# Context matmuls of a sliding-block attention kernel: streaming 194 columns instead of 193

## Chip, cores and metric

One core of one Trainium2 chip runs the whole program. The metric is the device time of one execution in microseconds; the kernel before takes 921.08 us (median of three runs, 920.9 to 921.36).

## The reference

A layer norm feeds two branches, attention against a cache (32 heads of 192, the last 512 cached positions) and a gated feed-forward block; their product is added to the input.

```python
W = min(4096, max(256, Sk // 4))                      # 512
q = (x @ wq).reshape(B, Sq, 32, 192).transpose(0, 2, 1, 3)
k, v = k_cache[:, :, Sk - W:, :], v_cache[:, :, Sk - W:, :]
scores = einsum("bhqd,bhkd->bhqk", q, k) * 192 ** -0.5
p = softmax(scores)
o = einsum("bhqk,bhkd->bhqd", p, v)                    # the context product
s = o.transpose(0, 2, 1, 3).reshape(B, Sq, 32 * 192) @ wo
...
return x + s * silu(((silu(xn @ w_gate)) * (xn @ w_up)) @ w_down)
```

## The kernel before

Heads are worked in 16 pairs. The softmax is not normalised until after the context product. The V tile has a column of ones behind the 192 columns of each head, so that the same matmul that forms the context also forms the sum of the row; the context is then divided by it. The tile has two columns of ones (194 columns per head), but only the first is streamed: 193 columns.

```python
V_p = consts.tile([P, KC, 2, Dh + 2], bf, name="V_p")      # KC = 4 chunks of 128 rows, 2 heads
...
nc.gpsimd.memset(V_p[:, :, :, Dh : Dh + 2], 1.0)           # once; the loads fill 0:Dh
...
def part(p):                                               # pairs 0 to 13: two 64-row halves at a time
    ...
    for kc in range(KC):
        for n, r in enumerate((lo, hi)):                   # rows 0-63 and 64-127 of the array
            k = n ^ turn
            qt = 2 * q2 + k
            m = nc.tensor.matmul(                          # L487
                acc[:, k, h * 256 : h * 256 + Dh + 1],
                Ps[i][kc][r, h, qt * P : (qt + 1) * P], V_p[r, kc, h, 0 : Dh + 1],
                start=(p == 0 and kc == 0), stop=(turn == 1 and kc == KC - 1),
                skip_group_check=True,
            )
...
def divide(i, q2, acc, by_dve):
    a_v = acc[:, :, :].rearrange("p k (h c) -> p k h c", h=2)
    nc.vector.reciprocal(r[:], a_v[:, :, :, Dh : Dh + 1])  # column 192
    ...                                                    # columns 0 to 191, scaled by r
...
def pv_full(i, q2):                                        # pairs 14 and 15: the full array
    ...
    nc.tensor.matmul(                                      # L539
        acc[:, k, h * 256 : h * 256 + Dh + 1],
        Ps[i][kc][:, h, qt * P : (qt + 1) * P], V_p[:, kc, h, 0 : Dh + 1],
        start=(kc == 0), stop=(kc == KC - 1),
    )
```

The softmax here doesn't subtract the row's maximum and nothing guards it: scores larger than these inputs give would overflow.

## Time and profile before

| | before |
|---|---|
| time | 921.08 us |
| matmul engine busy | 914.2 us, 99% of the span |
| context matmuls | 3584 of 64 rows (1792 side-by-side pairs) and 256 of 128 rows: 2048 slots |
| one slot, start to start | 83.5 ns |
| their share of the chain | 16% and 2% |

The prediction below shows the lines. A "slot" is the word used throughout for the time that one full matmul, or one pair of 64-row matmuls, holds the array. It is read from start times: from the start of a stretch of context matmuls to the start of whatever the engine does next, divided by the slots in between. Single start times stand in the trace to 1 ns; the timeline view rounds them to 10 ns. Unless said otherwise, a slot below is the median over all stretches of a kind. The tables of slots and gaps are worked out from these single start times; no view of the profile prints them, and differences under 1 ns do not show in the timeline lines of a short stretch.

### The profile page before, as it was taken

What the parts mean: (1) busy time and instruction counts of PE and PEld (TensorE: products, weight loads), DVE (VectorE), ACT (ScalarE), POOL (GpSimd) and SP (SyncE); (2) the same over time, 40 slices, a digit from 0 to 9 for tenths busy, and PEclk for the clock granted to TensorE, in tenths of its full rate; (3) what the DMA queues carried; (4) which work ended last, traced back from release to release, by engine and by line L of the source; (5) the groups of instructions that cost most, each with busy time, mean ns of one, the idle gap of its engine ahead of it and who ended that gap; (6) DMA issues with size and microseconds to landing.
All of it is one profiled execution on the core that took longest, in us unless ns stands there. A gap on an engine that the chain in (4) does not pass through costs nothing.

```text
span 919.1 us, 23174 instructions
## 1 busy us (share of the span) xinstructions
PE 914.2 (99%) x9920; PEld 548.9 (60%) x9920; DVE 601.8 (65%) x844; ACT 473.9 (52%) x840; POOL 85.2 (9%) x269
## 2 busy tenths in 40 slices
PE   9999999999999999999999999999999999999998
PEld 6444444465757575656565656566666666665665
DVE  6443321467677777777777777676867777777657
ACT  4222222557464646565656565655555555556471
POOL 0000000000000000000000000000000000001976
PEclk9999999999999999999999999999999999999999
DMA  9412430045352534253534343435243444443525
GB/s 299 79 35 64 92 82 0 1 75 112 54 113 50 111 51 108 54 108 54 108 58 109 57 108 52 110 53 108 56 87 73 90 77 75 91 71 102 120 59 166
DMA packets 248167, 77.53 MB, mean 84 GB/s; under 512 B 228993, under 2 KB 248065, under 8 KB 248065
## 3 DMA queue, kind: packets, MB, share of 16 engines
q1 hardware_dynamic: 245696, 73.39, 38.9%
q10 hardware_dynamic: 2368, 2.67, 0.9%
q8 instruction: 77, 1.26, 0.6%
q14 instruction: 26, 0.20, 0.1%
HBM read 38.93 MB, written 2.62 MB: 45 GB/s over the span
## 4 chain that ended last, share of the span: by engine, by line
PE 99%; DMA 1%; DVE 0%; ACTq 0%; issue 0%
PE mm L448 22%; PE sc L462 18%; PE mm L487 16%; PE sc L602 15%; PE sc L282 11%; PE mm L312 6%; PE sc L572 4%; PE sc L564 2%; PE mm L539 2%; PE mm L564 1%; DMA x_t<-in_A_x_dram 1%; PE gu L282 0%; PE mm L321 0%; PE sc L487 0%; PE sc L539 0%; PE mm L462 0%
## 5 line engine op out<-in xcount | busy, mean ns | idle before, releaser
L466 ACT ACTIVATE p_t<-sc 128x1024 bf16<-128x1024 f32 x254 | 252.9, 1022 | 120.5 <-PE sc L462 120.5
L453 DVE TENSOR_REDUCE qT<-mm 128x512 bf16<-128x1024 f32 x189 | 231.1, 1223 | 99.0 <-PE mm L448 96.5
L517 ACT ACTIVATE O_b<-mm,r 128x192 bf16<-128x192 f32 x486 | 164.6, 421 | 183.7 <-issue 136.9
L448 PE MATMUL mm<-xnT,wq_p 64*128 64x512 bf16 x1890 | 237.5, 376 | 0.0
L462 PE MATMUL sc<-qT,khat 64*128 64x512 bf16 x1524 | 198.0, 376 | 0.0
L487 PEld LDWEIGHTS <-p_t 64*128 64x128 bf16 x3584 | 159.3, 93 | 33.8
L487 PE MATMUL mm<-V_p,p_t 64*128 64x193 bf16 x3520 | 176.7, 242 | 0.0
L615 DVE TENSOR_TENSOR s_m<-s_m,sc 128x1024 f32<-128x1024 f32 x108 | 131.9, 1221 | 60.7 <-PE sc L602 52.3
L602 PE MATMUL sc<-wo_p,OT_b 64*128 64x512 bf16 x1296 | 168.8, 376 | 0.0
L448 PEld LDWEIGHTS <-wq_p 64*128 64x128 bf16 x1890 | 105.0, 94 | 98.9 <-issue 0.8
L462 PEld LDWEIGHTS <-khat 64*128 64x128 bf16 x1536 | 85.3, 94 | 80.4 <-DVE s_t L615 0.3
L602 PEld LDWEIGHTS <-OT_b 64*128 64x128 bf16 x1296 | 70.1, 94 | 44.1 <-issue 0.3
L615 DVE TENSOR_TENSOR s_t<-s_t,sc 128x512 f32<-128x512 f32 x108 | 74.2, 687 | 28.4 <-PE sc L572 26.6
L589 POOL MEMSET turn_t<- 128x1 f32 x220 | 21.6, 98 | 700.2 <-PE mm L487 506.2
L290 DVE TENSOR_TENSOR hT<-sc,sg 128x512 bf16<-128x512 f32 x46 | 31.7, 692 | 81.5 <-ACT sg L289 81.5
L289 ACT ACTIVATE sg<-sc 128x512 bf16<-128x512 f32 x46 | 27.3, 596 | 69.8 <-PE sc L282 69.8
L282 PE MATMUL sc<-xnT,wu_sb 128*128 128x512 bf16 (+1 forms) x260 | 60.5, 355 | 0.0
L282 PE MATMUL sc<-xnT,wg_sb 128*128 128x512 bf16 (+1 forms) x260 | 60.3, 355 | 0.1
L572 PE MATMUL sc<-OT_b,wo_p 64*128 64x512 bf16 (+1 forms) x345 | 50.3, 376 | 0.0
L312 PE MATMUL mm<-wd_sb,hT 128*128 128x512 bf16 x192 | 43.9, 379 | 0.0
L282 PEld LDWEIGHTS <-wu_sb 128*128 128x128 bf16 x285 | 27.2, 98 | 26.8 <-issue 0.2
L282 PEld LDWEIGHTS <-wg_sb 128*128 128x128 bf16 x285 | 27.2, 98 | 26.3
(83 smaller groups left out, 418.8 us busy)
## 6 DMA issues: line engine op xcount, KB each, us to landing
wo_p<-in_A_wo_dram SPq DMA_DIRECT2D x16, 480.0 KB, 4.8
K_p<-in_A_k_cache_dram SPq DMA_DIRECT2D x32, 192.0 KB, 4.6
V_p<-in_A_v_cache_dram SPq DMA_DIRECT2D x32, 192.0 KB, 3.6
wq_p<-in_A_wq_dram SPq DMA_DIRECT2D x64, 80.0 KB, 2.9
wq_p<-in_A_wq_dram SPq DMA_DIRECT2D x16, 160.0 KB, 3.2
x_t<-in_A_x_dram SPq DMA_DIRECT2D x13, 160.0 KB, 3.2
x_b<-in_A_x_dram SPq DMA_DIRECT2D x4, 512.0 KB, 6.4
OT_b<-O_b SPq DMA_TRANSPOSE x124, 2.8
```

Source lines behind the costliest of these rows:

```text
L282: nc.tensor.matmul(out, w_sb[:, c, f * P : (f + 1) * P], xnT[:, c, qc], start=(c == 0), stop=(c == NC - 1),)
L290: nc.vector.tensor_tensor(hTs[b][:, f, :], u, sg[:], ALU.mult)
L312: nc.tensor.matmul(dn, at, by, start=(f == 0), stop=(f == NF - 1))
L448: nc.tensor.matmul(q_ps[:, h, :], pairs[pr]["wq"][r, c, j * P : (j + 1) * P], xnT[r, c, b * 512 : (b + 1) * 512], start=(c == 0), stop=(c ...
L453: nc.vector.reduce_sum(qTs[i][:, j, :], q_ps[:, :, :].rearrange("p h n -> p n h"), axis=AX.X)
L462: nc.tensor.matmul(sc[:, h, :], khat[r, j, ks], qT[r, j, :], start=(j == 0), stop=(j == 2))
L466: nc.scalar.activation(p_t[:, :, :], sc[:, :, :], ACT.Exp, scale=scale)
L487: m = nc.tensor.matmul(acc[:, k, h * 256 : h * 256 + Dh + 1], Ps[i][kc][r, h, qt * P : (qt + 1) * P], V_p[r, kc, h, 0 : Dh + 1], start=(p ...
L517: nc.scalar.activation(O_b[:, qt, h, :], a_k[:, h, 0:Dh], ACT.Copy, scale=r[:, k, h, :])
L572: nc.tensor.matmul(ps.rearrange("p (t q) -> p t q", q=P), pairs[i // NB]["wo"][r, j, MC:D], OTs[i][:, :, :].rearrange("p (t j) q -> p j t ...
L602: m = nc.tensor.matmul(ps[:, k, :], OTs[i][r, 3 * (2 * half + k) + j, :], pairs[i // NB]["wo"][r, j, MAIN], start=(turn == 0 and j == 0), ...
L615: nc.vector.tensor_tensor(to, to, ps, ALU.add)
```

## The change

The intent is to stream both columns of ones, so that the width is even. The second one is computed and never read.

```diff
-                        acc[:, k, h * 256 : h * 256 + Dh + 1],
-                        Ps[i][kc][r, h, qt * P : (qt + 1) * P], V_p[r, kc, h, 0 : Dh + 1],
+                        acc[:, k, h * 256 : h * 256 + Dh + 2],
+                        Ps[i][kc][r, h, qt * P : (qt + 1) * P], V_p[r, kc, h, 0 : Dh + 2],
...   (the same two lines in pv_full)
```

More of the change, by code (lines that the diff above doesn't have):

```diff
@@ L539, in pv_full @@
                     nc.tensor.matmul(
-                        acc[:, k, h * 256 : h * 256 + Dh + 1],
-                        Ps[i][kc][:, h, qt * P : (qt + 1) * P], V_p[:, kc, h, 0 : Dh + 1],
+                        acc[:, k, h * 256 : h * 256 + Dh + 2],
+                        Ps[i][kc][:, h, qt * P : (qt + 1) * P], V_p[:, kc, h, 0 : Dh + 2],
                         start=(kc == 0), stop=(kc == KC - 1),
```

## The prediction

> **What bounds the kernel now.** I read the page first: the busy shares, the clock row, and the chain of work that ended last.
>
> ```profile
> PE 914.2 (99%) x9920; PEld 548.9 (60%) x9920; DVE 601.8 (65%) x844; ACT 473.9 (52%) x840; POOL 85.2 (9%) x269
> ...
> PEclk9999999999999999999999999999999999999999
> ...
> PE 99%; DMA 1%; DVE 0%; ACTq 0%; issue 0%
> PE mm L448 22%; PE sc L462 18%; PE mm L487 16%; PE sc L602 15%; PE sc L282 11%; PE mm L312 6%; PE sc L572 4%; PE sc L564 2%; PE mm L539 2%; PE mm L564 1%; DMA x_t<-in_A_x_dram 1%; PE gu L282 0%; PE mm L321 0%; PE sc L487 0%; PE sc L539 0%; PE mm L462 0%
> ```
>
> The reader is to see three things. The matmul engine is busy 99% of the span at full granted clock, so its cycles are the time. The chain says the same independently of busy time: 99% of the end-to-end path is matmul followed by matmul. And the two lines that the change edits, L487 (row-tiled context product) and L539 (full-array context product of the last two head pairs), are 16% and 2% of that path. There is nothing to hide a longer matmul behind, and nothing that would swallow a shorter one. So the question is only how long one of these matmuls holds the array at 193 columns and at 194.
>
> Next the groups of instructions with shapes kept apart, for counts.
>
> ```profile
> L487 PE MATMUL mm<-V_p,p_t 64*128 64x193 bf16 x3520 | 176.7, 242 | 0.0
> L539 PE MATMUL mm<-V_p,p_t 128*128 128x193 bf16 x224 | 20.8, 246 | 0.0
> L487 PE MATMUL sc<-V_p,p_t 64*128 64x193 bf16 x64 | 3.3, 242 | 0.0
> L539 PE MATMUL sc<-V_p,p_t 128*128 128x193 bf16 x32 | 2.8, 246 | 0.0
> L487 PEld LDWEIGHTS <-p_t 64*128 64x128 bf16 x3584 | 159.3, 93 | 33.8
> ```
>
> L487 runs 3520 + 64 = 3584 times, always as two 64-row halves side by side, that is 1792 pairs; L539 runs 224 + 32 = 256 times. That makes 1792 + 256 = 2048 slots of the array. The 242 and 246 ns are one instruction's time from start to its modelled end and overlap with the next, so they are not the price of a slot. The price is start to start, which I take from the timeline of the matmul engine (first column start, second length, both in us).
>
> ```profile
> 885.23 2.84 PE L539 MATMUL mm<-V_p,p_t 128*128 128x193 bf16 x32
> 887.91 2.83 PE L539 MATMUL sc<-V_p,p_t 128*128 128x193 bf16 x32
> 890.58 1.50 PE L539 MATMUL mm<-V_p,p_t 128*128 128x193 bf16 x16
> 891.92 1.46 PE L564 MATMUL sc<-wo_p,OT_b 128*128 128x512 bf16 x6
> ```
>
> ```profile
> 282.52 0.85 PE L487 MATMUL mm<-V_p,p_t 64*128 64x193 bf16 x16
> 283.19 1.47 PE L602 MATMUL sc<-wo_p,OT_b 64*128 64x512 bf16 x12
> ...
> 285.79 1.51 PE L487 MATMUL mm<-V_p,p_t 64*128 64x193 bf16 x32
> 287.13 0.83 PE L572 MATMUL sc<-OT_b,wo_p 64*128 64x512 bf16 x6
> ```
>
> Full array: 891.92 - 885.23 = 6.69 us for 80 matmuls, 83.6 ns each. Row pairs: 287.13 - 285.79 = 1.34 us for 16 pairs, about 83.75 ns each at this rounding. Single start times in the trace are finer: nearly every stretch of 16 full matmuls or 16 pairs takes 1336 ns and every stretch of 8 pairs 668 or 669 ns, so a slot is 83.5 ns, the same in both forms.
>
> For comparison the timeline gives other widths on the full array.
>
> ```profile
> 150.75 5.34 PE L312 MATMUL mm<-wd_sb,hT 128*128 128x512 bf16 x24
> 155.93 1.24 PE L321 MATMUL mm<-xnT,wq_p 128*128 128x512 bf16 x5
> ...
> 910.16 0.49 PE L564 MATMUL mm<-wo_p,OT_l 128*128 128x256 bf16 x3
> ...
> 915.08 0.49 PE L564 MATMUL sc<-wo_p,OT_b 128*128 128x256 bf16 x3
> ```
>
> 512 columns: 5.18 us / 24 = 215.8 ns. 256 columns: 4.92 us over fifteen groups of three, 109.3 ns (the finer starts mostly read 109). The slope is (215.8 - 109.3) / 256 = 0.416 ns a column, with about 2.5 ns per matmul on top (215.8 - 512 x 0.4167 = 2.5).
>
> **What the Trainium skill says.** "TensorE: Matmul & The Clock Gate", section "Wait — 56ns, not 53.3ns?", gives start to start of back-to-back matmuls at full clock as N / 2.4 GHz plus about 2.5 ns. The trace agrees at 512 (215.8 against 215.8) and 256 (109.2 expected, 109.3 read). At 193 it does not quite: 80.4 + 2.5 = 82.9 ns expected, 83.5 measured. The section "Back-to-back issue gap" of the same page offers about 131 ns per matmul as a sustained rate at N = 512; no full-array matmul here does that, so I don't use it.
> "PSUM — Partial Sum Buffer", section "Specifications (TRN2)", lists cachelines of 8 bytes, which is two fp32 output columns. No run here shows that yet, but it would make 193 columns, 772 bytes, end in a half-filled line, and 194 in a full one.
>
> The fine structure at 193 fits some such unevenness. In the stretch at 890.58 the starts stand at .581, .663, .749, .832, .914, .997 and 1.083: gaps of 82, 86, 83, 82, 83, 86 ns. Every fourth gap is some 4 ns longer, and the other three are slightly shorter than 82.9. The 512-column stretches show only 215 and 216. Four slots take 4 x 83.5 = 334 ns, in 2.4 GHz cycles 802, or 200.4 per slot: 193 plus 7.4, where the widths above cost N plus 6. A 194-column matmul at the plain rate would take 194 + 6 = 200 cycles, 83.33 ns. So 193 already pays for 194, and a little more.
>
> **The change part by part.** It removes nothing and adds no instruction: every instruction stays in its place on every engine, and only the names of the 193-wide matmuls become 194. The second ones column already exists (the tile has 194 columns per head and the memset fills both), so no load or memset grows. The output gains a column at 193 within each head's 256-column half bank, which nobody reads: the reciprocal reads column 192, the scaled copies 0 to 191. ScalarE, VectorE and the DMAs are unchanged, and so are the waits, since the semaphores sit on the same matmuls. LDWEIGHTS is unchanged: 3584 loads take 159.3 us, 44 ns each as a union, 89 ns for two, yet they overlap the streaming, and the matmuls show no idle time before them (0.0 in the last column).
>
> Cost: 2048 slots on the path. By the plain rate against what is measured at 193: 83.33 - 83.5 = -0.17 ns, times 2048 = -0.35 us. This is my main case: a change of about -0.04%, indistinguishable from nothing in a total that spread from 920.9 to 921.36 over three runs.
>
> **The rivals.**
> (1) Pure streaming: each column costs its 0.417 ns, and whatever makes 193 slow stays. Then 2048 x 0.417 = +0.85 us, 921.9. For it speaks the slope between 256 and 512; against it that 193 is already off that line by 0.6 ns, more than the price of a whole column.
> (2) The irregular fourth gap has to do with the width not being a multiple of four, and 194 shows it every second matmul. If a 4 ns hiccup came every second slot rather than every fourth, it would add 4 / 4 = 1 ns per slot, about +2 us, together with the column +2.9 us: 924. For it speaks the period of four; against it that the mean excess at 193 is small, as if the long gap repaid the three short ones rather than being a stall on top.
> (3) The opposite: odd widths cost more than I can see, and an even one falls under the plain rate. The floor is the streaming itself, 194 / 2.4 = 80.8 ns, so at most 2.7 ns x 2048 = -5.5 us (-0.6%). Nothing speaks for it, as no width in the trace beats N plus 6 cycles on average.
> (4) A new bound, LDWEIGHTS or a wait for a PSUM buffer: the loads do not change, and the readers of the accumulator start at most one column, 0.4 ns, later. I give it nothing.
>
> No rival reaches 2%: 2% is 18.4 us, 9 ns per slot, or 22 columns' worth.
>
> **Range and chances.** Main case 920.7 at about 55%, rival 1 921.9 at about 30%, rival 2 up to 924 at about 10%, rival 3 the rest. Their weighted centre is about 921.2, and I put the point at 921.0, a little nearer the main case. The range must also hold run-to-run and chip-to-chip differences of perhaps half a microsecond, so 919.9 to 922.3. Chances: faster by over 2% 0.01, within 2% 0.98, slower by over 2% 0.01.
>
> **What would show it.** In the profile of the changed kernel, the stretch of 80 matmuls of L539 should take 6.67 us (80 x 83.33), where it takes 6.69 now; pure streaming would show 6.72. At single start times, a stretch of 16 full matmuls should take 1333 ns (pure streaming 1343), and gaps should read 83 and 84 with no longer one every fourth. The busy sums of L487 are a bad judge, since they include modelled ends. The chain should still be 99% matmul with L487 at 16%. I would be wrong if 194-wide slots came out at 84 ns or more, if a long gap appeared every second slot, or if the order or the waits at the reciprocal changed. A total above 923 or below 919 would mean a mechanism that I have not seen.

## The result

The changed kernel takes 921.06 us (median of six runs, 920.84 to 921.58), the kernel before 921.16 us beside it (six runs, 920.78 to 922.33). The ratio is 0.9998 with a 95% interval of 0.9985 to 1.0011: the same. Ratios here and below are the mean time of one kernel's fast runs over that of the other's of the same rounds, so not quite the ratio of the medians quoted.

The page of the changed kernel: busy times, and the chain that ended last.

```profile
PE 912.4 (99%) x9898; PEld 548.3 (60%) x9920; DVE 601.5 (65%) x844; ACT 473.9 (52%) x840; POOL 85.2 (9%) x269
...
PE 99%; DMA 1%; issue 0%; SPq 0%; DVE 0%
```

The bound has not moved. The 914.2 us before and 912.4 us here are not a gain: the records of 22 matmuls are missing from this trace (9898 against 9920), and the span is 919.2 us against 919.1.

The groups with shapes kept apart, then the timeline of the matmul engine (start and length in us):

```profile
L487 PE MATMUL mm<-V_p,p_t 64*128 64x194 bf16 x3520 | 176.7, 242 | 0.0
L539 PE MATMUL mm<-V_p,p_t 128*128 128x194 bf16 x224 | 20.8, 246 | 0.0
```

```profile
285.85 1.51 PE L487 MATMUL mm<-V_p,p_t 64*128 64x194 bf16 x32
287.19 0.83 PE L572 MATMUL sc<-OT_b,wo_p 64*128 64x512 bf16 x6
...
885.29 2.84 PE L539 MATMUL mm<-V_p,p_t 128*128 128x194 bf16 x32
887.97 2.83 PE L539 MATMUL sc<-V_p,p_t 128*128 128x194 bf16 x32
890.64 1.50 PE L539 MATMUL mm<-V_p,p_t 128*128 128x194 bf16 x16
891.97 1.46 PE L564 MATMUL sc<-wo_p,OT_b 128*128 128x512 bf16 x5
```

The same counts and busy times with 194 in place of 193. Sixteen pairs take 287.19 - 285.85 = 1.34 us, as before. The eighty full matmuls take 6.68 us in this view; from single start times it is 6.685 us here and 6.686 us before. Stretches of 16 slots have the median 1336 ns in both kernels. Summed from single starts over all context stretches, it is 171.05 us in both. So a slot is 83.5 ns at 194 as at 193: the added column costs nothing that these traces can show. And the long gap is still there: the first gaps of a stretch of full matmuls read 84, 86, 82, 83, 82, 87, 82 ns.

This leaves two questions for experiments. Why is the column free: do widths count in twos, or does something else hide it? And what makes the slot 83.5 ns rather than the 83.33 ns of the prediction's main case, if 194 does not cure it?

The theories: **A**, widths count in pairs of columns, and the slot is the even width over 2.4 GHz plus 2.5 ns. **B**, a granule (the number of columns that are counted together) larger than two. **C**, plain streaming, 0.42 ns for each column, with the 194th hidden by something in these kernels. **D**, for the 0.17 ns and the long gap alone: the start addresses of successive reads of the V tile.

### The profile page after: what moved, and what is told of

Its sections match the earlier page's. It is cut to its first block, busy times and chain, and to the rows that moved or that the text cites. A ratio compares the mean times of both kernels' runs of the same rounds, so it can differ in the third digit from the quotient of the medians.

```text
span 919.2 us, 23152 instructions
## 1 busy us (share of the span) xinstructions
PE 912.4 (99%) x9898; PEld 548.3 (60%) x9920; DVE 601.5 (65%) x844; ACT 473.9 (52%) x840; POOL 85.2 (9%) x269
## 4 chain that ended last, share of the span: by engine, by line
PE 99%; DMA 1%; issue 0%; SPq 0%; DVE 0%
PE mm L448 22%; PE sc L462 18%; PE mm L487 16%; PE sc L602 15%; PE sc L282 11%; PE mm L312 6%; PE sc L572 4%; PE sc L564 2%; PE mm L539 2%; PE mm L564 1%; DMA wg_sb<-in_B_w_gate_dram 1%; PE gu L282 0%; PE mm L321 0%; PE sc L539 0%; PE sc L487 0%
## 5 line engine op out<-in xcount | busy, mean ns | idle before, releaser
L487 PE MATMUL mm<-V_p,p_t 64*128 64x194 bf16 x3520 | 176.7, 242 | 0.0
L462 PEld LDWEIGHTS <-khat 64*128 64x128 bf16 x1536 | 85.3, 94 | 80.4 <-DVE s_t L615 0.3
```

Of the source, the lines that this page charges most:

```text
L462: nc.tensor.matmul(sc[:, h, :], khat[r, j, ks], qT[r, j, :], start=(j == 0), stop=(j == 2))
L487: m = nc.tensor.matmul(acc[:, k, h * 256 : h * 256 + Dh + 2], Ps[i][kc][r, h, qt * P : (qt + 1) * P], V_p[r, kc, h, 0 : Dh + 2], start=(p ...
```

## The experiments

Several kernels give each of the 16 head pairs another width or layout, so one trace holds a whole sweep: 128 slots for each pair. The V tile is declared flat for this, with room for 256 columns per head; one of three buffers of an unrelated tile at the end of the kernel was given up for the space, and the ones are written anew when the layout changes. These kernels' totals are mixtures with added waits and are not compared; only their slots are used.

```diff
-    V_p = consts.tile([P, KC, 2, Dh + 2], bf, name="V_p")
+    PLAN = [(256, 0, 193), (256, 0, 194), ...]   # distance of V rows, columns ahead of the first, columns streamed
+    V_p = consts.tile([P, 2048], bf, name="V_p")
+    def V_of(pr):
+        st, off, _ = PLAN[pr]
+        return V_p[:, off : off + KC * 2 * st].rearrange("p (k h d) -> p k h d", k=KC, h=2)
...
-                        acc[:, k, h * 256 : h * 256 + Dh + 1],
-                        Ps[i][kc][r, h, qt * P : (qt + 1) * P], V_p[r, kc, h, 0 : Dh + 1],
+                        acc[:, k, h * 256 : h * 256 + PLAN[pr][2]],
+                        Ps[i][kc][r, h, qt * P : (qt + 1) * P], V_of(pr)[r, kc, h, 0 : PLAN[pr][2]],
...
-            s_f = finp.tile([P, 2, MC], f32, name="s_f", bufs=3)
+            s_f = finp.tile([P, 2, MC], f32, name="s_f", bufs=2)
```

### Widths from 193 to 256, V rows 256 columns apart

> Each head pair streams another width (193 to 256 columns), all from a V tile whose rows start 256 columns apart, so every read starts at the same alignment; the answers stay right. Slots (start to start on the array) are read pair by pair. Theory A, widths count in twos: 193 and 194 both 83.3 ns, 195 and 196 both 84.2, 198 85.0, 200 85.8, 208 89.2, 224 95.8, 240 102.5, 256 109.2. Theory B, a granule of 8 columns: 193 to 200 all about 85.8 or all about 83.5, then a step of 3.3 ns to 202. Theory C, plain streaming of one column per cycle: 193 at 82.9, 194 at 83.3, 195 at 83.75, 0.42 ns more each.

The kernel's answer was right. Slots by width:

| columns | 193 | 194 | 195 | 196 | 197 | 198 | 200 | 202 | 204 | 208 | 212 | 216 | 224 | 240 |
|---|---|---|---|---|---|---|---|---|---|---|---|---|---|---|
| slot, ns | 83.4 | 83.4 | 84.2 | 84.2 | 85.0 | 85.0 | 85.9 | 86.6 | 87.5 | 89.1 | 90.8 | 92.5 | 95.9 | 102.5 |

Each of the three odd widths costs what the next even one costs, and a pair of columns costs 0.83 ns, two cycles of 2.4 GHz. All values lie within 0.1 ns of (even width) / 2.4 + 2.5. Theory B falls, as the 195th column is not free. Theory C falls too: the 195th costs 0.8 ns, two columns' worth, and the 196th again nothing. Here, with rows 256 columns apart, the long fourth gap is absent (gaps 83, 83, 84, 83, 83, 84), which already points at D.

### Width 193, V rows at different distances

The edit is the plan alone: distances 193 to 256, width 193 throughout.

> Width 193 throughout, but each head pair keeps its V rows another distance apart (193 to 256 columns), so the start addresses of successive matmuls differ. Theory A (the half-filled output line at the end of 193 columns sets the price): 83.3 to 83.5 ns at every distance, and the long gap on every fourth matmul stays. Theory D (the start addresses in the V tile set it): 83.5 with the long fourth gap at 194, where the starts step by 8 bytes modulo 64; no long gap and 82.5 to 83.0 ns at 208, 224, 240 and 256, where all four starts of a head are equally aligned; something else at 193, 195 and 197, whose second head starts 2 bytes off a word.

The kernel's answer was right.

| distance, columns | 193 | 194 | 195 | 196 | 197 | 198 | 200 | 202 | 204 | 208 | 216 | 224 | 240 | 256 |
|---|---|---|---|---|---|---|---|---|---|---|---|---|---|---|
| slot, ns | 83.9 | 83.5 | 83.9 | 83.4 | 83.7 | 83.6 | 83.3 | 83.6 | 83.4 | 83.3 | 83.4 | 83.3 | 83.4 | 83.3 |
| long gap, one in | uneven | 4 | uneven | 8 | uneven | 3 or 5 | none | 4 | 8 | none | none | none | none | none |

The excess over 83.33 belongs to the distance of the rows and not to the width: theory D, in part. The control is the first distance of the plan, 194, which reads 83.5 as in the kernel before. At multiples of 8 columns (16 bytes) all gaps are 83 or 84 ns. At 196 and 204, where successive chunks of one head lie a multiple of 16 bytes apart and the two heads do not, there is one long gap per eight slots, at the first chunk of the second head (85.9 ns on average), and the average is hardly raised. My expectation of 82.5 to 83.0 ns at 208 and beyond was wrong: the floor is 83.33, that of 194 columns, as theory A has it.

### All context matmuls at 256 columns

Against the two kernels above the edit is the plan alone: every pair streams 256 columns. Against the kernel before it has their other changes too.

> Every context matmul streams 256 columns instead of 193. All theories hold the slots to be on the path: 2048 slots x (109.2 - 83.5) ns = +52.6 us, 973.7 us in all, a ratio of 1.057. If the loads of the weights or a hidden wait set the slot at 193, so that width does not matter near 194, the total would grow by less than this.

The kernel's answer was right; 973.76 us (four runs, 973.48 to 974.42) beside 921.01 us, ratio 1.0569 (1.0552 to 1.0587). The group of the row-tiled matmuls and a stretch of the timeline:

```profile
L499 PE MATMUL mm<-V_p,p_t 64*128 64x256 bf16 x3520 | 219.4, 269 | 0.0
```

```profile
935.27 3.67 PE L551 MATMUL mm<-V_p,p_t 128*128 128x256 bf16 x32
938.77 3.66 PE L551 MATMUL sc<-V_p,p_t 128*128 128x256 bf16 x32
942.26 1.91 PE L551 MATMUL mm<-V_p,p_t 128*128 128x256 bf16 x16
944.01 1.46 PE L576 MATMUL sc<-wo_p,OT_b 128*128 128x512 bf16 x6
```

Eighty full matmuls now take 8.74 us, 109.25 ns each, and no idle time stands before them. The expected 973.7 us was met. By single starts the context stretches alone grow from 171.05 to 223.60 us, +52.55 us, so they account for the whole +52.75 us of the total within its interval, and the other changes for next to nothing. So all 2048 slots lie on the path, and a longer slot has no slack outside in which to hide: the 194th is free because the slot itself does not grow. Whether a load of the weights sets a floor inside the slot, this kernel cannot tell; the 192 columns below can.

### The whole tile shifted, and 192 columns

Distance 256, width 193, the tile shifted by 0 to 32 columns per pair; the last two pairs stream 192 columns and divide by the wrong column.

> Width 193, V rows 256 columns apart, and each head pair shifts the whole tile by another number of columns (0, 1, 2, 3, 4, 6, 8, 12, 14, 16, 20, 24, 28, 32), so all its reads start equally far off a 64-byte line. The last two pairs stream 192 columns and divide by the wrong column: their part of the answer is wrong on purpose. Theory A: all 83.3 to 83.5 ns, no dependence on the shift; 192 columns at 82.5. Theory D: the slot depends on the shift, lowest at 0 and 32; it may rise by up to some 4 ns where a read crosses one more line.

The result was wrong (relative error 0.73). At all even shifts (0, 2, 4, 6, 8, 12, 14, 16, 20, 24, 28, 32) the slot is 83.3 to 83.4 ns with even gaps. At shifts of 1 and 3 columns it is 84.1 ns, one pair of columns more. The 192 columns of the last pairs:

```profile
885.97 2.81 PE L551 MATMUL mm<-V_p,p_t 128*128 128x192 bf16 x32
888.62 2.80 PE L551 MATMUL sc<-V_p,p_t 128*128 128x192 bf16 x32
891.26 1.48 PE L551 MATMUL mm<-V_p,p_t 128*128 128x192 bf16 x16
892.58 1.46 PE L576 MATMUL sc<-wo_p,OT_b 128*128 128x512 bf16 x6
```

6.61 us for eighty, 82.6 ns (82.5 as the median of stretches): one pair less than 193, as A expects. This also answers a rival to A, that the weight loads set the slot: at 93 and 97 ns each by the profile they are longer than a slot, and overlap each other and the matmuls. But a slot set by them would not shrink with the 193rd column, nor step up at the 195th. In its simple form D falls: an even shift of all reads by the same number of columns, a multiple of 16 or 64 bytes or not, costs nothing. What remains of D is the change of the start from one read to the next. Neither theory had the cost of an odd start of the read.

### The output shifted

To see at which end the pairs are counted, the output's start in its half bank was shifted too. The readers follow.

```diff
-                        acc[:, k, h * 256 : h * 256 + Dh + 1],
+                        acc[:, k, h * 256 + TO[pr] : h * 256 + TO[pr] + PLAN[pr][2]],
...
-        a_v = acc[:, :, :].rearrange("p k (h c) -> p k h c", h=2)
+        a_v = acc[:, :, :].rearrange("p k (h c) -> p k h c", h=2)[:, :, :, TO[pr] :]
```

> V rows 256 columns apart; by head pair, the output starts 0 to 3 columns further on in its half bank, or the reads start 0 to 3 columns further on in the V tile, at widths 193 to 196; the readers follow, so the answer stays right. If the pairing comes from the output[...], then 194 columns written from an odd column span 98 lines and cost 84.2 ns where 83.3 at even ones, and 195 from an odd column 84.2, 196 from an odd column 85.0. If it comes from the stream that is read or counted, the output's start changes nothing (194: 83.3 at every output start), and only odd read starts cost a pair more: 194 at 84.2, 195 at 84.2 or 85.0, 196 at 85.0, whatever the output's start.

The kernel's answer was right.

| read starts at column | output starts at column | 193 columns | 194 | 195 | 196 |
|---|---|---|---|---|---|
| even | even | 83.4 (above) | 83.3 | 84.2 | 84.2 (above) |
| even | 1 | 83.3 | 84.1 | 84.2 | 84.9 |
| even | 3 | | 84.1 | | |
| 1 or 3 | even | 84.1 (above) | 84.1 to 84.2 | 84.9 | 85.0 |
| 1 | 1 | 83.3 | 84.1 | | |

With the read at an even column, the slot follows the number of aligned pairs of output columns that the output touches: 194 columns from column 1 touch 98 pairs and cost what 196 cost, 193 columns from column 1 touch 97 and cost what 194 cost. So the pairing does show at the output. An odd read against an even output costs a further pair; where both are odd, the count is that of the output again. I had put the two ends against each other, and both take part. The trace cannot tell whether the memory's lines or the array's own paths make the pairs.

### Whole kernels with rows 200 columns apart

The V tile is 200 columns per head instead of 194, which fits without giving up a buffer; the widths are 193, 194 and 196.

```diff
-    V_p = consts.tile([P, KC, 2, Dh + 2], bf, name="V_p")
+    V_p = consts.tile([P, KC, 2, 200], bf, name="V_p")
...
-        nc.gpsimd.memset(V_p[:, :, :, Dh : Dh + 2], 1.0)
+        nc.gpsimd.memset(V_p[:, :, :, Dh:200], 1.0)
```

> The whole kernel at width 193 with V rows 200 columns apart: slots of 83.33 ns without the long fourth gap, where before has 83.5. In time 2048 x -0.17 = -0.35 us, a ratio of 0.9996: a gain only the slots can show, not the total. The rival, that the long gaps repay themselves elsewhere, has the slots at 83.5 on average.

> The same at width 194: slots of 83.33 ns again, as 193 counts as 194; the total like that at 193. Plain streaming would have 0.42 ns more per slot, +0.85 us.

> The same at width 196, two columns past 194: one more pair, slots of 84.17 ns, 2048 x (84.17 - 83.33) = +1.7 us over 194 at the same row distance, and +1.4 us over before, a ratio of 1.0015. If the next columns are free too (a granule of more than two, off the critical path), the total stays at that of 194.

All three gave the right answer. Slots are means over the row-tiled stretches. Beside 921.38 us of the kernel before (nine runs, 920.74 to 922.03):

| kernel | median, us (runs) | ratio to before | slot, ns |
|---|---|---|---|
| rows 200 apart, 193 columns | 920.52 (5) | 0.9992 (0.9980 to 1.0005) | 83.33 |
| rows 200 apart, 194 columns | 920.84 (5) | 0.9995 (0.9981 to 1.0008) | 83.33 |
| rows 200 apart, 196 columns | 922.30 (5) | 1.0016 (1.0003 to 1.0028) | 84.17 |

The timeline at 194 and at 196 columns:

```profile
884.62 2.84 PE L539 MATMUL mm<-V_p,p_t 128*128 128x194 bf16 x32
887.30 2.83 PE L539 MATMUL sc<-V_p,p_t 128*128 128x194 bf16 x32
889.97 1.50 PE L539 MATMUL mm<-V_p,p_t 128*128 128x194 bf16 x16
891.30 1.46 PE L564 MATMUL sc<-wo_p,OT_b 128*128 128x512 bf16 x5
```

```profile
886.25 2.87 PE L539 MATMUL mm<-V_p,p_t 128*128 128x196 bf16 x32
888.96 2.86 PE L539 MATMUL sc<-V_p,p_t 128*128 128x196 bf16 x32
891.65 1.51 PE L539 MATMUL mm<-V_p,p_t 128*128 128x196 bf16 x16
893.00 1.46 PE L564 MATMUL sc<-wo_p,OT_b 128*128 128x512 bf16 x5
```

Eighty slots take 6.68 us and 6.75 us in this view (6.677 us at 194 columns by single starts, against 6.685 in the changed kernel). Summed from single starts over all context stretches, 171.05 us before become 170.69 us at 194 columns, -0.36 us, and 172.39 us at 196, +1.70 us over that. The first was expected as -0.35, the second as +1.7. Part of the -0.36 us comes back: the 512-column output matmuls between the stretches take 1295 ns per twelve where they took 1294, some 0.1 us in all. A version with rows 200 apart is the best that I have, but its total is not clear of the noise; the slots alone show the gain. The 196-column kernel is the one whose total moves clear of it: +0.92 us over the kernel before by the medians, and by the ratio of 1.0016 about the +1.4 us (1.0015) that was expected, though far under 2%. The price of one pair of columns over 2048 slots is real, and the change did not pay it.

### The order of the chunks

Width 194 and distance 194, as in the changed kernel; each pair takes its four chunks in another order.

```diff
-            for kc in range(KC):
+            for kc in ORDER[pr]:
...
-                        start=(p == 0 and kc == 0), stop=(turn == 1 and kc == KC - 1),
+                        start=(p == 0 and kc == ORDER[pr][0]), stop=(turn == 1 and kc == ORDER[pr][-1]),
```

> Width 194 and rows 194 columns apart as in the changed kernel, but each head pair takes its four 128-row chunks in another order (sums are the same up to rounding). If the long gap belongs to a pair of start addresses, it moves with the chunks: in the cyclic order 1, 2, 3, 0 it comes first instead of second, in 3, 0, 1, 2 third, and other orders (3, 2, 1, 0 or 0, 2, 1, 3) have another number of long gaps or none; the slot may move between 83.33 and some 84.5 ns. If it belongs to the second place of each group of four, whatever is read, it stays second in every order and all slots read 83.5.

The kernel's answer was right. The long gaps move with the chunks. In the order 0, 1, 2, 3 the second gap of each four is the long one; in 0, 2, 1, 3 the third (86.0 ns on average for the first head, 86.4 for the second); in 0, 3, 1, 2 the second again, now behind chunk 3; in 1, 2, 3, 0 the first and third share it (84.5 and 85.1) for the first head and the second head has 85.3 at its first. In all ten orders the longest gaps stand behind chunk 1 or chunk 3. Those are the chunks whose starts lie 8 bytes off those of chunks 0 and 2, modulo 16. The slot stays at 83.5 to 83.6 ns in every order, so none of these ten orders repairs it; a distance that is a multiple of 8 columns does. So the place in the group of four alone does not decide it. Nor does every change of the start bring a long gap: in the order 0, 1, 2, 3 it changes at every slot, and one gap in four is long. My expectation was right only in part: in the orders 1, 2, 3, 0 and 3, 0, 1, 2 (84.5, 83.1, 84.9 and 82.5 ns for the first head) the long gap does not move whole, it splits. Why such a change of the start makes one gap some 86 ns long and leaves the next three at 82.5, 0.8 ns under the average of even rows, the trace does not say, and it stays open.

## Why the prediction was right, and where it was off

- **The bound.** All 2048 slots are on the path: shown by the 256-column kernel (+52.75 us by the medians, for +25.7 ns per slot).
- **"193 already pays for 194."** The mechanism was right, and it is shown: widths count in pairs of output columns, so 193 and 194 are the same slot. The half-filled pair at the end, inferred before from an 8-byte line, is what the sweep and the shifted output show; that it is PSUM's line is not shown.
- **"And a little more", with 194 at 83.33 ns, -0.35 us.** This step failed. The extra 0.17 ns is not a property of width 193 but of V rows 194 columns apart, which the change leaves alone. So the slot stayed at 83.5 ns, the long gap every fourth slot stayed, and the expected -0.35 us is 0 (171.05 us of context stretches before and after). By the prediction's own sign, a stretch of 16 had to fall from 1336 to 1333 ns; it did not. The prediction took two irregularities for one because the kernel before shows them only together. The 0.35 us exists, and rows 200 apart collect about that in the context stretches.
- **Rival 1, +0.85 us,** fell: the slot did not grow by 0.42 ns. The 0.42 ns per column is right only as an average over the two columns of a pair.
- **Rival 2, a stall tied to the width modulo four,** fell: at 194 the period is still four, and it follows the addresses.
- **Rival 3, an even width below the plain rate,** fell: no even width was below it.
- **The total and the chances.** 921.06 us lies where the prediction put it (921.0, 919.9 to 922.3), but a total with this spread could not have told the main case from rival 1; the slots did. That the point came within 0.06 us is luck: it was a weighted middle between cases, none of which came true as written, and the median of the kernel before alone read 921.01 to 921.38 us from one set of rounds to the next.

## What to carry to other kernels

Where the matmul engine is the bound, price a width by start-to-start times in the trace, and ask first whether the next column crosses a pair: with an even start, an odd width can take one more column for nothing, while trimming one pays only where it empties a pair. Keep reads and outputs at even columns, and give rows of the streamed tile a distance that is a multiple of 16 bytes where the space is there; padding of 6 columns removed the uneven slots here. All this was measured with bf16 reads, fp32 outputs and widths of 192 to 256. When one measurement shows two irregularities together, change one of them alone before using their sum.

## What the Trainium skill lacked or had wrong

- "TensorE: Matmul & The Clock Gate", section "Wait — 56ns, not 53.3ns?": start to start as N / 2.4 GHz plus about 2.5 ns holds here for even N only. Odd N counts as N + 1: 193 reads 83.4 ns (82.9 by the formula) with rows 256 columns apart, 195 reads 84.2, 197 reads 85.0.
- The same page has nothing on where operands start: with an odd start of the output, 194 columns cost 84.1 instead of 83.3 ns; with an odd start of the read alone, 193 cost 84.1 instead of 83.4.
- No page has the effect of the distance between successively streamed rows: 83.5 ns and a long gap every fourth slot at 194 columns, 83.33 ns and even gaps at 200.
- "SBUF — State Buffer", section "Operand start alignment", says of its own runs that they timed nothing; the matmul reads at odd columns here give the right answer, and cost 0.8 ns each where the output starts at an even column (84.1 against 83.3 or 83.4 ns at 193).
- "PSUM — Partial Sum Buffer", section "Specifications (TRN2)", lists 8-byte cachelines without a price for touching one more: 0.83 ns per pair of fp32 columns in these slots. That the pairs are these lines, no run shows.
- "TensorE: Matmul & The Clock Gate", section "Back-to-back issue gap", gives about 131 ns per matmul as the sustained rate at N = 512; full-array matmuls here read 215.8 ns.
